# A gated recurrence feeding an ELU layer: ELU and denominators moved into PSUM, and a new order of all operations

## The chip, the cores and the metric

The kernel runs on one core of a Trainium2 chip. The time is device microseconds of one execution. Engines are named as the profile names them: PE is TensorE's matmuls (PEld its weight loads), DVE is VectorE, ACT is ScalarE, POOL is GpSimd, SP issues the DMAs. PSUM is the memory that PE writes; DVE and ACT read and write it, POOL never appears with a PSUM operand in this kernel.

## The reference

Two parts follow each other. First a recurrence over 768 steps for 4 batches and 8 heads of width 40, then a feed-forward layer with ELU on the result (3072 rows of 320).

```
for t in range(S):
    m_new = max(f[t] + m, i[t])
    C = exp(f[t] + m - m_new) * C + exp(i[t] - m_new) * outer(v[t], k[t])
    n = exp(f[t] + m - m_new) * n + exp(i[t] - m_new) * k[t]
    m = m_new
    y[t] = sigmoid(o[t]) * (C @ q[t]) / max(abs(n @ q[t]), 1)
h = x @ w_in                                  # x is y, [3072, 320]; w_in [320, 2048]
g = where(h > 0, h, exp(min(h, 0)) - 1)       # ELU
out = g @ w_out                               # [2048, 320]
```

## The kernel before, in words

The recurrence is computed in chunks. A tile is one batch and 128 steps, so there are 24 tiles, numbered n. For a tile, DVE scans the gates into decay weights (`ws`, line 509), PE multiplies keys and queries into the PSUM tile `pa` (`kq`, line 527) and forms the new state there (`us`, line 538), the weights and the product are multiplied (`wp`, 553), the state C is shrunk and added to (`shrink` 565, `gather` 571), and PE sums the outputs into the PSUM tile `pb` (`y`, line 587). Four multiplications with both inputs in SBUF prepare this: `va` (477), `kw` (513), `qb` (548, 551) and `shrink` (565). Each may stand on DVE or on POOL.

Then comes the denominator chain of a tile, on 128x8 elements: `den` takes the absolute value from `pb` (616 on ACT, 618 on DVE), `recip` inverts it (622), `half` caps it (624, DVE or POOL), `oscale` multiplies the output gate by it (626, DVE), and `result` multiplies `pb` by that into `xf` (632). PE turns `xf` (`turn`, 651) and ACT and DVE split it into an upper part `xh` (654) and a rest `xl` (656). In the kernel before, the denominators lie in two SBUF tiles, `den`.

The feed-forward layer works on blocks of two tiles (256 rows). The 2048 columns are taken 256 at a time, which makes a group: h is 128x512 in one of two PSUM banks `ph`. PE forms it with 16 matmuls (line 690), ACT writes relu(-h) and exp of it into the SBUF tile `e` (698, 700), DVE makes the ELU of it (`elu`, 702), a copy rounded to the narrower type goes to `gh` (line 201 on ACT, DVE or POOL), the rest to `gl` (707, DVE or POOL), and 12 matmuls (717) sum gh and gl times the second weights into the banks `pc`. There are 97 groups, two of them half as wide. There are 2 `e`, 3 `gh` and 2 `gl` tiles.

The weights arrive as 64-bit words and are split by a chain of DVE, ACT and POOL operations (lines 294 to 339, `join` on POOL at 325), 18 conversions in all, beside the first tiles.

Every operation is recorded by name with what it reads and writes. The table `PLACES` holds one number for each operation, its place in the order, and a letter (p, v, a, g, s for PE, DVE, ACT, POOL, SP) where it does not stand on the first engine of its list. Operations are issued in that order, so that each engine runs its own in that order, and waits come from what is read and written.

Of the kernel before, what the change touches and what calls it, by code (L numbers as in the profile page):

```python
# [11 lines left out]
F32 = mybir.dt.float32  # L12
F32R = mybir.dt.float32r
AF = mybir.ActivationFunctionType
ALU = mybir.AluOpType
# [12 lines left out]
    9g 39 0 10 3 4 5 20 30 13 59 62 61 65 64 69 73 79 2 31 46 35 48 41 51 63v 75 33 28 102v 104 92 106 105 109 116  # L28
# [13 lines left out]
    162 161 152 147 142 192 188 224v 212 199 216g 222 228 246 258 242v 254 266v 297 264 279v 281 283g 288 300 302a  # L42
    305 322 333 245 240 198 205 236 203 248 276 329 294 306 309 313 321 326 314v 331 367v 375 339 351v 354 356g
    358 361 363a 369 372 381 201 269 384g 388g 360g 400 418 373 420 442 447 489 473 390 415a 392 399 408 412 421
    452 470 492 499 406 413 432 436 458 478 483g 503 513 430 435 482 487 496 501 507 519 522 469 484 495 498 502
    516g 520 545 550 571 574 568 736 251 318 253 315 239 328 320 355v 376 368 377g 383 387 411 404 380 393 405 409
    417 426 427 429g 431 434 438a 441 448 455 342 337 330 323 335 403 394 402v 480 414 422g 423 425 466 449 450
    456 530v 536 475 488v 490 491 494 500 504 510 514 518 526 529 538 541 547 553 570 578 584 535 542 546 549 552
    562v 575 593 597 554 559 583 586 596 599 606 626 630 564 572 580 589 598 617 624 635 639 661 666 652v 835 600
    609 620 634 638 640 651g 685 691 616 623 645 647 650 665 688g 698 705 656 664 675 679 692 714 727 785 789 671  # L50
    680 693 696 699 723 732 794 800 764 812 840 718 808 832 709 719 740 749 756 788g 796 821 827 738 745 751 753
    769 795 811g 833 838 763 768 801 805 810 813 848 853 869 777 782 819 822 841 844 858 872 875 859 882 884 857
    880 943 816 842 851 870 874 876v 878g 892 896 846 849 863 867 877 883g 886g 899 902 881 885 894 898 901 906v
# [771 lines left out]
```

## Time and profile before

| what | us |
|---|---|
| median of 3 runs | 483.02 |
| lowest and highest run | 481.78, 485.48 |
| the profiled execution, its own time | 480.93 |
| span of its trace | 479.1 |

The trace is of the profiled execution. Its span leaves out 1.83 us of that execution's own time, and the median of the runs is 2.09 us above it. A busy PE in the profile is not PE at its peak, because the records of matmuls that wait in its queue overlap.

### The profile page before, as it was taken

The page shows a single profiled execution, that of the slowest core. Times are in us where ns is not written, and L with a number is a line of the kernel's source. Part 1 is how long each engine was busy: PE and PEld are TensorE (multiplying, and loading weights), DVE is VectorE, ACT ScalarE, POOL GpSimd, SP SyncE. Part 2 cuts the span into 40 slices and gives each one's busy share as a digit, 9 for nine tenths or more (in the row PEclk, how much of TensorE's full clock was granted, in tenths as well). Part 3 has the DMA queues.
Part 4 walks back from the last instruction along what each step waited for, and adds up shares of the span by engine and source line. Part 5 has one row for each costly group of instructions (what it writes and reads, how often), then busy time and mean ns, then how long its engine had stood idle before and what let it go on. Part 6 is the DMA issues. An engine that isn't in the chain of part 4 may idle for free.

```text
span 479.1 us, 14899 instructions
## 1 busy us (share of the span) xinstructions
PE 451.7 (94%) x6414; PEld 430.6 (90%) x6414; DVE 304.9 (64%) x570; ACT 224.5 (47%) x431; POOL 149.7 (31%) x167
## 2 busy tenths in 40 slices
PE   5888999998797899999999999999999999999996
PEld 2557989897797899999999999999999999999996
DVE  6868998998999665555744574464554663533342
ACT  4356896686755323434544244244342524234342
POOL 3334333453334314023132420402431424232121
PEclk9999999999997999999999999999999999999999
DMA  8963867494756250423433322016025100000000
GB/s 238 297 167 113 228 176 207 140 263 143 218 145 175 57 161 29 102 70 79 119 101 81 97 80 72 30 33 171 1 71 152 63 30 1 30 1 1 29 1 27
DMA packets 23139, 50.34 MB, mean 105 GB/s; under 512 B 4490, under 2 KB 10826, under 8 KB 23074
## 3 DMA queue, kind: packets, MB, share of 16 engines
q1 hardware_dynamic: 23074, 49.40, 36.7%
q8 instruction: 50, 0.82, 0.7%
q14 instruction: 15, 0.12, 0.1%
HBM read 43.32 MB, written 6.06 MB: 103 GB/s over the span
## 4 chain that ended last, share of the span: by engine, by line
PE 69%; DVE 4%; issue 3%; ACT 1%; POOL 0%; DVEq 0%; POOLq 0%; ACTq 0%
PE ph L690 32%; PE pc L717 29%; PE pb L587 4%; PE pa L527 2%; PE pa L538 2%; PE pb L651 1%; DVE e L702 1%; DVE gl L707 1%; DVE w L509 0%; DVE vko L513 0%; DVE vko L626 0%; DVE w L339 0%; ACT e L700 0%; POOL C L565 0%; DVE va L477 0%
## 5 line engine op out<-in xcount | busy, mean ns | idle before, releaser
L690 PE MATMUL ph<-xh,w 128*128 128x256 f32 x960 | 187.7, 288 | 1.3 <-DVE e L702 1.3
L717 PE MATMUL pc<-w,gh 128*128 128x320 f32 x768 | 172.1, 311 | 0.0
L690 PEld LDWEIGHTS ph<-xh,w 128*128 128x128 f32 x960 | 150.0, 194 | 2.7 <-DVE e L702 1.6
L717 PEld LDWEIGHTS pc<-w,gh 128*128 128x128 f32 x768 | 126.5, 188 | 0.5
L690 PE MATMUL ph<-xl,w 128*128 128x256 f32 x576 | 124.8, 285 | 0.0
L702 DVE SCALAR_TENSOR_TENSOR e<-e,ph 128x512 f32<-128x512 f32 (+1 forms) x97 | 65.5, 678 | 90.9 <-ACT e L700 90.7
L717 PE MATMUL pc<-w,gl 128*128 128x320 f32 x384 | 118.7, 309 | 0.4 <-DVE gl L707 0.4
L698 ACT ACTIVATE e<-ph 128x512 f32<-128x512 f32 (+1 forms) x97 | 57.1, 591 | 128.0 <-PE ph L690 110.8
L690 PEld LDWEIGHTS ph<-xl,w 128*128 128x128 f32 x576 | 97.8, 194 | 0.0
L717 PEld LDWEIGHTS pc<-w,gl 128*128 128x128 f32 x384 | 72.1, 188 | 0.7 <-DVE gl L707 0.7
L707 POOL TENSOR_TENSOR gl<-e,gh 128x512 fp32r<-128x512 f32 (+1 forms) x36 | 47.9, 1332 | 65.1 <-PE pc L717 29.4
L700 ACT ACTIVATE e<-e 128x512 f32<-128x512 f32 (+1 forms) x97 | 60.3, 627 | 2.4
L707 DVE TENSOR_TENSOR gl<-e,gh 128x512 fp32r<-128x512 f32 (+1 forms) x61 | 45.0, 739 | 12.2 <-POOL gh L201 3.8
L325 POOL TENSOR_TENSOR narrow<-narrow,wide 128x512 int32<-128x512 int32 (+1 forms) x18 | 27.4, 1522 | 49.7 <-ACT wide L313 18.6
L201 ACT CAST gh<-e 128x512 fp32r<-128x512 f32 (+1 forms) x48 | 29.3, 611 | 27.4 <-DVE e L702 23.8
L201 POOL CAST gh<-e 128x512 fp32r<-128x512 f32 (+1 forms) x27 | 19.3, 714 | 64.6 <-DVE e L702 62.2
L587 PE MATMUL pb<-va,w 64*32 64x41 f32 (+1 forms) x1440 | 25.3, 205 | 2.2 <-issue 2.2
L509 DVE TENSOR_TENSOR_SCAN w<-w,ones 128x512 f32<-128x512 f32 x20 | 24.5, 1228 | 2.7 <-DMA w<-f_d 2.7
L656 DVE TENSOR_TENSOR xl<-pb,xh 128x384 fp32r<-128x384 f32 x24 | 13.3, 554 | 19.0 <-ACT xh L654 19.0
L587 PEld LDWEIGHTS pb<-va,w 64*32 64x32 f32 (+1 forms) x1440 | 21.6, 112 | 3.7 <-issue 2.5
L654 ACT CAST xh<-pb 128x384 fp32r<-128x384 f32 x24 | 11.4, 474 | 27.1 <-PE pb L651 14.8
L527 PEld LDWEIGHTS pa<-qk 40*64 40x64 f32 x768 | 15.4, 145 | 8.4 <-issue 5.1
(92 smaller groups left out, 444.7 us busy)
## 6 DMA issues: line engine op xcount, KB each, us to landing
vko<-in_vko SPq DMA_DIRECT2D x24, 480.0 KB, 5.4
qk<-in_qk SPq DMA_DIRECT2D x44, 192.0 KB, 5.4
wide<-in_w_out SPq DMA_DIRECT2D x8, 640.0 KB, 5.9
w<-f_d SPq DMA_DIRECT2D x40, 128.0 KB, 3.5
wide<-in_w_in SPq DMA_DIRECT2D x8, 512.0 KB, 4.1
out<-os SPq DMA_DIRECT2D x24, 160.0 KB, 3.3
bb<-b_d SPq DMA_DIRECT2D x37, 96.0 KB, 3.4
sum<-os SPq DMA_DIRECT2D x12, 160.0 KB, 4.6
```

Of the source, the lines that this page charges most:

```text
L201: nc.scalar.copy(o, i) if e == "ACT" else eng[e].tensor_copy(o, i)
L325: lambda e: nc.gpsimd.tensor_add(word, word, high if by_act else low),
L509: lambda e: nc.vector.tensor_tensor_scan(flat, src, ones.rearrange("p h t -> p (h t)"), 0.0, op0=ALU.mult, op1=ALU.add),
L527: nc.tensor.matmul(pp()[HALF[s], two, j, :], kt[rows, j, HALF[s]], qt[rows, j, HALF[s]], start=True, stop=True, skip_group_check=True)
L587: nc.tensor.matmul(y[at, two, j, :], a, m, start=(at.start, two) not in begun, stop=False, skip_group_check=True)
L656: lambda e: nc.vector.tensor_sub(xl[j][:, :, ts], tp, xh[j][:, :, ts].bitcast(F32)),
L690: nc.tensor.matmul(h, a[g][:, cols], m, start=(i == 0), stop=(i == len(prods) - 1), skip_group_check=True)
L698: lambda e, h=h, ev=ev: nc.scalar.activation(ev, h, AF.Relu, scale=-1.0), KHP, (KE,))
L700: lambda e, ev=ev: nc.scalar.activation(ev, ev, AF.Exp, scale=-1.0), (), (KE,))
L702: lambda e, h=h, ev=ev: nc.vector.scalar_tensor_tensor(out=ev, in0=ev, scalar=-1.0, in1=h, op0=ALU.add, op1=ALU.max),
L707: lambda e, gh=gh, gl=gl, ev=ev: eng[e].tensor_sub(gl, ev, gh.bitcast(F32)),
L717: nc.tensor.matmul(pc[a][:, 0:DM], x[:, sl], bw[g][:, j, :], start=(f == f0 and part == 0), stop=(f == f1 - 1 and part == 2))
```

## The change

Three things are changed. The ELU is written over h in PSUM instead of into `e`, and `gh` and `gl` are made from there, so that neither can stand on POOL. The denominators lie in eight columns of `pb` instead of SBUF, so that `half` can't stand on POOL either; `pb` is declared as one row of 1024 columns for that, with the same addresses for all that was in it. [...]

```diff
 PLACES = """
-    9g 39 0 10 3 4 5 20 30 13 59 62 61 65 64 69 73 79 2 31 46 35 48 41 51 63v 75 33 28 102v 104 92 106 105 109 116
+    3g 6 0 4 9v 25 17 7 5 29 48 67 59 73 70 75 80 89 36 92v 94 84 96 95 100 108 117 43 38 113 120 115 122 118 124
...
-    pb = psum.tile([P, 2, 512], F32, name="pb")
+    pb = psum.tile([P, 1024], F32, name="pb")
...
-        den, xf = dens[n % room["den"]], xfs[n % room["xf"]]
-        KDN, KXF = ("den", n % room["den"]), ("xf", n % room["xf"])
+        den, xf = pb[:, 896 : 896 + H].rearrange("p (a j) -> p a j", a=2), xfs[n % room["xf"]]
+        KDN, KXF = ("den", 0), ("xf", n % room["xf"])
...
-        op(f"half {n}", "DVE POOL",
-           lambda e: eng[e].tensor_scalar(den, den, 1.0, 0.5, op0=ALU.min, op1=ALU.mult), (), (KDN,))
+        op(f"half {n}", "DVE",
+           lambda e: nc.vector.tensor_scalar(den, den, 1.0, 0.5, op0=ALU.min, op1=ALU.mult), (), (KDN,))
...
             op(f"elu {label}", "DVE",
                lambda e, h=h, ev=ev: nc.vector.scalar_tensor_tensor(
-                   out=ev, in0=ev, scalar=-1.0, in1=h, op0=ALU.add, op1=ALU.max),
-               KHP, (KE,))
-            op(f"gh {label}", "ACT DVE POOL", lambda e, gh=gh, ev=ev: copy(e, gh, ev), (KE,), (KG,))
-            op(f"gl {label}", "DVE POOL",
-               lambda e, gh=gh, gl=gl, ev=ev: eng[e].tensor_sub(gl, ev, gh.bitcast(F32)),
-               (KE, KG), (KL,))
+                   out=h, in0=ev, scalar=-1.0, in1=h, op0=ALU.add, op1=ALU.max),
+               (KE,), KHP)
+            op(f"gh {label}", "ACT DVE", lambda e, gh=gh, h=h: copy(e, gh, h), KHP, (KG,))
+            op(f"gl {label}", "DVE",
+               lambda e, gh=gh, gl=gl, h=h: nc.vector.tensor_sub(gl, h, gh.bitcast(F32)),
+               KHP + [KG], (KL,))
```

With the new letters, of the 97 groups DVE makes gl for all (61 before, POOL 36) and gh for 37 (22 before), ACT gh for 60 (48 before) and POOL none (27 before). POOL's list falls from 171 rows to 91, DVE's grows from 572 to 636.

The first place is DVE at the denominators of tile 8. `den_112` is an SBUF tile, `pb` and `ph` are PSUM, `e`, `gh`, `gl` and `vko` are SBUF. Before:

```order
L618 TENSOR_SCALAR den_112<-pb 128x8
L622 RECIPROCAL den_112<-den_112 128x8
L624 TENSOR_SCALAR den_112<-den_112 128x8
L626 SCALAR_TENSOR_TENSOR vko_106<-vko_106,den_112 128x320
L702 SCALAR_TENSOR_TENSOR e_123<-e_123,ph_147 128x512
L632 TENSOR_TENSOR xf_114<-pb,vko_106 128x320
L702 SCALAR_TENSOR_TENSOR e_124<-e_124,ph_148 128x512
L707 TENSOR_TENSOR gl_128<-e_123,gh_126 128x512
```

And in the changed kernel, at the same rows of the list:

```order
L618 TENSOR_SCALAR pb<-pb 128x8
L622 RECIPROCAL pb<-pb 128x8
L624 TENSOR_SCALAR pb<-pb 128x8
L299 TENSOR_SCALAR narrow_98<-narrow_98 128x512
L626 SCALAR_TENSOR_TENSOR vko_106<-vko_106,pb 128x320
L632 TENSOR_TENSOR xf_112<-pb,vko_106 128x320
L571 TENSOR_TENSOR C_85<-C_85,pa 104x164
L707 TENSOR_TENSOR gl_126<-ph_145,gh_124 128x512
```

The scaling of the gate and the rest of a group each had two SBUF inputs and now have one; the rest follows the denominators with other work between.

The second place is POOL in the stage of the first tiles. `vko_...<-vko,w` is kw, `C<-C,bb` is shrink, `qk<-bb,qk` is qb, `narrow` is join. Before:

```order
L513 TENSOR_TENSOR vko_106<-vko_106,w_109 128x320
L624 TENSOR_SCALAR den_111<-den_111 128x8
L325 TENSOR_TENSOR narrow_98<-narrow_98,wide_94 128x512
L565 TENSOR_TENSOR C_85<-C_85,bb_92 104x164
L325 TENSOR_TENSOR narrow_97<-narrow_97,wide_95 128x512
L707 TENSOR_TENSOR gl_129<-e_124,gh_125 128x512
L325 TENSOR_TENSOR narrow_98<-narrow_98,wide_96 128x512
L201 COPY xf_114<-xf_114 128x64
L201 CAST gh_127<-e_124 128x512
```

And in the changed kernel, as far into the conversions:

```order
L512 TENSOR_TENSOR vko_106<-vko_106,w_109 128x320
L382 TENSOR_TENSOR fi_100<-fi_100,mx 32x128
L324 TENSOR_TENSOR narrow_98<-narrow_98,wide_94 128x512
L201 COPY xf_111<-xf_111 128x64
L565 TENSOR_TENSOR C_85<-C_85,bb_92 104x164 x2
L324 TENSOR_TENSOR narrow_97<-narrow_97,wide_95 128x512
L551 TENSOR_TENSOR qk_89<-bb_92,qk_89 104x512
L512 TENSOR_TENSOR vko_107<-vko_107,w_110 128x320
L476 TENSOR_TENSOR va_86<-vko_107,va_86 128x8x40
```

Denominators, rests and copies of groups have left POOL, and the multiplications of the recurrence (kw, shrink, qb, va) stand there in their stead.

The third place is PE at the tenth turn (line 651, tile 9). Lines 690 and 717 are the first and the second layer. Before:

```order
L690 MATMUL ph_147<-xh_116,w_67 128x256
L690 MATMUL ph_147<-xl_120,w_67 128x256 x2
L690 MATMUL ph_147<-xh_116,w_67 128x256 x3
L651 MATMUL pb<-ident,xf_114 128x128 x3
L527 MATMUL pa<-qk_89 64x64 x16
L538 MATMUL pa<-va_86,vko_106 64x41 x16
L690 MATMUL ph_148<-xh_116,w_67 128x256
```

And in the changed kernel:

```order
L717 MATMUL pc_147<-w_71,gh_125 128x320 x2
L717 MATMUL pc_147<-w_71,gl_127 128x320
L717 MATMUL pc_148<-w_71,gh_125 128x320 x2
L717 MATMUL pc_148<-w_71,gl_127 128x320
L538 MATMUL pa<-va_86,vko_106 64x41 x16
L651 MATMUL pb<-ident,xf_112 128x128 x3
L690 MATMUL ph_145<-xh_114,w_67 128x256
L690 MATMUL ph_145<-xl_118,w_67 128x256
```

A group of the first layer that stood ahead of the turn now stands behind it, and the state products of tile 10 (538), which stood behind it, stand ahead; their `kq` (527) stands a few rows further ahead.

## Rows read from the trace of the kernel before

**Rows 1.** The page: busy us, share and instructions; granted clock in 40 slices.

```profile
PE 451.7 (94%) x6414; PEld 430.6 (90%) x6414; DVE 304.9 (64%) x570; ACT 224.5 (47%) x431; POOL 149.7 (31%) x167
...
PEclk9999999999997999999999999999999999999999
```

**Rows 2.** Windows: length, busy us (and instructions) of PE, PEld, DVE, ACT, POOL; clock, DMA.

```profile
0.00:55.00 55.00, 43.52 (x665) 32.33 (x666) 42.79 (x89) 29.54 (x62) 19.93 (x27) 1.00 0.72 207
55.00:146.00 91.00, 84.50 (x1469) 80.07 (x1467) 86.51 (x155) 68.55 (x131) 35.78 (x35) 1.00 0.68 190
146.00:476.00 330.00, 323.69 (x4285) 318.18 (x4284) 175.61 (x328) 126.42 (x239) 93.97 (x106) 0.99 0.23 65
```

**Rows 3.** Timeline of DVE, the tenth xl (start, us, line, operation).

```profile
144.91 0.54 DVE L656 TENSOR_TENSOR xl<-pb,xh 128x384 fp32r<-128x384 f32 x1
```

**Rows 4.** Groups of DVE by form, 0 to 146 us: busy us, mean ns, idle before.

```profile
L702 DVE SCALAR_TENSOR_TENSOR e<-e,ph 128x512 f32<-128x512 f32 x20 | 13.4, 678 | 0.3 <-ACT e L700 0.2
L707 DVE TENSOR_TENSOR gl<-e,gh 128x512 fp32r<-128x512 f32 x17 | 12.7, 758 | 0.0
...
L626 DVE SCALAR_TENSOR_TENSOR vko<-vko,den 128x320 f32<-128x320 f32 x10 | 9.3, 933 | 0.8
L553 DVE TENSOR_TENSOR w<-pa,w 128x512 f32<-128x512 f32 x11 | 7.5, 685 | 1.3 <-PE pa L538 1.3
...
L339 DVE SCALAR_TENSOR_TENSOR w<-narrow,w 128x512 fp32r<-128x512 f32 x8 | 5.9, 737 | 0.0
...
L571 DVE TENSOR_TENSOR C<-C,pa 104x164 f32<-104x164 f32 x17 | 5.3, 313 | 0.7 <-PE pa L538 0.7
...
L477 DVE TENSOR_TENSOR va<-vko,va 128x320 f32<-128x320 f32 x10 | 4.8, 476 | 0.0
L300 DVE TENSOR_SCALAR narrow<-narrow 128x512 f32<-128x512 f32 x10 | 4.7, 468 | 0.0
L513 DVE TENSOR_TENSOR vko<-vko,w 128x320 f32<-128x320 f32 x7 | 4.3, 621 | 0.1
L551 DVE TENSOR_TENSOR qk<-bb,qk 104x512 f32<-104x512 f32 x5 | 3.4, 683 | 0.0
...
L565 DVE TENSOR_TENSOR C<-C,bb 104x164 f32<-104x164 f32 x8 | 3.1, 387 | 0.0
...
L624 DVE TENSOR_SCALAR den<-den 128x8 f32<-128x8 f32 x4 | 1.8, 458 | 0.1
...
L618 DVE TENSOR_SCALAR den<-pb 128x8 int32<-128x8 int32 x4 | 0.6, 160 | 2.4 <-PE pb L587 2.4
```

**Rows 5.** Tile den over the whole span: min/median/max ns, first and last start.

```profile
L626 DVE SCALAR_TENSOR_TENSOR vko<-vko,den x24: 484/493/2824, 18.8 to 433.8; 128x320 f32<-128x320 f32 x24
...
L624 DVE TENSOR_SCALAR den<-den x15: 161/172/1308, 18.5 to 433.3; 128x8 f32<-128x8 f32 x15
```

**Rows 6.** Groups of POOL, 0 to 146 us: busy us, mean ns, idle before.

```profile
L513 POOL TENSOR_TENSOR vko<-vko,w 128x320 f32<-128x320 f32 x5 | 5.9, 1183 | 6.9 <-DVE w L509 3.5 <-PE pb L651 3.3
```

**Rows 7.** Groups of ACT by form, whole span: busy us, mean ns, idle before.

```profile
L700 ACT ACTIVATE e<-e 128x512 f32<-128x512 f32 x95 | 59.4, 631 | 2.3
L698 ACT ACTIVATE e<-ph 128x512 f32<-128x512 f32 x95 | 56.3, 595 | 124.6 <-PE ph L690 107.7 <-DVE gl L707 7.4 <-issue 5.2
L201 ACT CAST gh<-e 128x512 fp32r<-128x512 f32 x47 | 28.9, 615 | 26.9 <-DVE e L702 23.3 <-PE pc L717 1.9 <-PE pb L587 1.5
```

**Rows 8.** The chain that ended last, in order of time: start, us, what.

```profile
177.07 0.62 PE pa L527 x32
177.70 0.45 PE pa L538 x32
...
188.67 3.84 PE ph L690 x32
192.51 3.52 PE pc L717 x24
```

**Rows 9.** Timeline of PE: the longest stop in its own issuing.

```profile
151.90 0.59 PE L527 MATMUL pa<-qk 40*64 40x64 f32 x11 [2.87 <-issue]
```

More of the change, by code (lines that the diff above doesn't have):

```diff
@@ new lines @@
+    1036 1038 1040 1044a 1046 1050 1055 690 772 775g 786g 782g 828 833 1052 839 840 844 841 911 1062 1088 1226
+    1230 1233 1234 1236 1238v 1241 1270 1273 1232 1242 1250 1252 1266 1268v 1272 1275 1283 1260 1263 1269 1271
+    1274 1276 1277 1288 1304 1278 1281 1284 1289 1291 1297 1302 1310 1320 1293 1300 1306 1308 1312 1316 1318 1324
+    1336 1314 1317 1321 1323 1325 1328 1330 1340 1343 1326 1329 1332 1333 1335 1338v 1341 1359 1364 1331 1334 1337
+    1339 1342 1344 1346 1370 1376 1382 1394 1384 1388 866 905 903 909 963 838 984 923v 1032 1009 1020 935 1025
@@ new lines @@
+    1494 1527 1569 1593 1607 1609 1610 1612 1615v 1618 1629 1635 1608 1611 1614 1616 1619 1623 1627 1659 1662 1620
+    1624 1631 1634 1636 1640v 1643 1664 1668 1644 1648 1652 1656 1661 1663v 1665 1671 1686 1651 1667 1669 1670
+    1672 1675 1681 1689 1701 1673 1676 1680 1684 1694 1697 1700 1704 1710 1693 1698 1702 1703 1705 1707 1709 1713
+    1723 1706 1708 1711 1712 1714 1716 1719 1725 1727 1731v 1734 1730 1732 1360 1389 1372 1377 1375 1292 1307
+    1449v 1547 1433 1460 1469 1471 1559 1557 1522v 1526 1575 1579 1580 1590 1591 1592 1595v 1598 1600 1638 1519
@@ new lines @@
+    1516 1431 1418 1485 1403 1401 1461v 1467 1501 1561 1573 1574 1603 1630 1429v 1576 1641 1645 1646 1647 1649
+    1650 1653v 1658 1660 1666 1715 1718 1721 1722 1724 1726v 1728 1739 1743 1720 1729 1735 1736 1738 1741v 1744
+    1746 1751 1733 1737 1740 1742 1747 1750v 1753 1756 1763 1748 1754 1757 1758 1760 1762 1764 1767 1775 1759 1761
+    1765 1766 1768 1771v 1773 1779 1784 1769 1772 1777 1782 1785 1788v 1791 1794 1801 1789 1792 1795 1796 1798
+    1800 1802 1805 1807 1797 1799 1803 1804 1806 1808v 1810 1812 1819 1824 1826 1823v 1828 1476 1528 1531 1483
@@ new lines @@
+    1480 1628 1525 1633v 1683 1554 1566 1637 1639 1642 1657 1654v 1655 1685 1687v 1688 1690 1691 1692 1695a 1696
+    1699 1745 1578 1586 1596 1582 1584 1632 1562 1677v 1717 1674 1678 1679 1682 1749 1755 1752v 1770 1774 1776
+    1778 1780 1781 1783 1786 1787 1790 1793 1809 1811 1813 1814 1816 1818 1820 1831 1835 1815 1817 1821 1825 1829
+    1830v 1833 1837 1839 1822 1827 1832 1834 1836 1838v 1840 1848 1851 1841 1842 1844 1845 1847 1849 1852 1854
+    1865 1843 1846 1850 1853 1855 1857v 1858 1869 1872 1856 1859 1861 1862 1864 1867v 1870 1874 1877 1860 1863
@@ L107 @@
+    1866 1868 1871 1873 1875 1883 1887 1876 1878 1879 1881 1882v 1884 1890 1880 1885 1886 1888 1889v 1891 1892
+    1894 1896 1893 1895
 """
@@ L193, in tile_mlstm_then_elu_ffn @@
     room = dict(
-        wide=3, narrow=2, gates=2, qk=3, bb=3, vko=3, w=3, den=2, xf=2, x=4, e=2, gh=3, gl=2, os=3,
+        wide=3, narrow=2, gates=2, qk=3, bb=3, vko=3, w=3, xf=2, x=4, e=2, gh=3, gl=2, os=3,
     )
@@ L234, in tile_mlstm_then_elu_ffn @@
     ws = tiles("w", P, H, Q)
-    dens = tiles("den", P, 2, HH)
     xfs = tiles("xf", P, 3 * P if XDUP else H * D)
@@ L519, in us @@
             return pa[:, s, HH * Q : HH * (Q + E)].rearrange("p (j e) -> p j e", e=E)
-        y = pb[:, :, 0 : HH * E].rearrange("p a (j e) -> p a j e", e=E)
+        part = pb[:, 0:1]
+        y = bass.AP(tensor=part.tensor, offset=part.offset, ap=[list(part.ap[0]), [512, 2], [E, HH], [1, E]])
         def products(e):
```

129 lines of the change are left out of this document (56 added, 73 removed), and 11 rows, old and new, of the table PLACES.

## The prediction, made before the changed kernel was run

> **What bounds the kernel now.** I read the page first, then windows by stage, then DVE's groups in the stage where DVE is full. The page has PE at 94% and DVE at 64% of the span [rows 1], which alone says that nothing on DVE matters. The windows say otherwise [rows 2]. Up to 55 us the first four tiles pass through a chain of all engines. From 55 to 146 us DVE is busy 86.51 of 91.00 us, so it idles 4.5 us in all: it is the engine that sets when this stage ends. From 146 to 476 us PE is busy 323.69 of 330.00 us and DVE only 175.61: PE sets the pace there. So time can be won in two places only: by DVE's queue up to some 146 us, and by PE's few stops behind. As the mark at which the first stage ends I take the tenth xl (tile 9): it starts at 144.91 us and lasts 0.54 [rows 3], so it ends at 145.5; the span ends 333.6 us later.
>
> What fills DVE ahead of the mark is in rows 4. The oscale instruction (line 626) stands out: 933 ns in the mean of ten, where the median over the whole trace is 493 and the longest 2824 [rows 4, 5]. Its inputs are both in SBUF, and so are those of gl (line 707), 758 ns, while wp (line 553), of the same size with one input in PSUM, takes 685 and elu (line 702) 678. I read the long ones as DVE waiting for POOL, which works beside it on SBUF.
>
> **The change, part by part, up to the mark.** The sum is made against the profiled execution.
>
> 1. Long instructions that become short. With the denominators in PSUM, oscale has one SBUF input left, gl has one, and half (line 624) none. I price each at its undisturbed time: oscale 10 x (933 - 493) = 4.4 us; gl 17 x (758 - 685) = 1.2; half 4 x (458 - 172) = 1.1 [rows 4, 5]. Together 6.8 us to rounding. Below, the gain is 0, if the same waiting moves to DVE's other instructions; above, it is what else waits besides, some 0.5 us for line 339 (8 x (737 - 678) by elu's time of the same width) [rows 4]. I take 6.8, since the forms with a PSUM input are even: 678 and 685 are within 1% of each other.
>
> 2. Work moved from DVE to POOL ahead of the mark, counted in the two orders: va 10 to 4, kw 7 to 2, qb 7 to 4, shrink 10 to 4. At the rows' means that is 6 x 0.476 + 5 x 0.621 + 3 x 0.683 + 6 x 0.387 = 10.3 us less [rows 4].
>
> 3. Work moved to DVE or drawn ahead of the mark: half 4 to 10 (6 x 0.172 = 1.0), den 4 to 7 (0.5), gl 17 to 19 (1.4), two instructions of the setup that POOL did (1.4, at line 553's 685 each), hi 1 to 3 and clip 17 to 18 (3 x 0.468 = 1.4), lo 18 to 19 (0.7), wp 10 to 11 (0.7), gather 16 to 18 (0.6), one gh that reads PSUM (0.3 more); elu goes 20 to 19 (0.7 less) [rows 4, 5]. That is 7.3 us more. A few gate operations also leave DVE; they would only add to the gain, and I leave them out. With step 2: 3.0 us less.
>
> 4. Writing to PSUM with DVE occurs nowhere in the trace: elu, recip, half and den now do it. Reading PSUM costs nothing that the rows show (553 against 551, 685 to 683 [rows 4]). Below I put no cost. Above, each of the 46 instructions ahead of the mark that now write there (19 elu, 7 den, 10 recip, 10 half) is longer by a whole small instruction, 160 ns (line 618) [rows 4]: 7.4 us. I take 0, the row nearest by form being the reading one. [...] A dear PSUM is a rival below.
>
> 5. PE. Ahead of the tenth turn stand 336 matmuls of line 690 and 216 of 717 before, and 320 and 216 now; one tile's kq and us have come ahead instead. At 3.84 us for 32 of line 690, and 0.62 + 0.45 for kq and us [rows 8], PE has 1.92 - 1.07 = 0.85 us more left behind the mark.
>
> 6. What is late next. When DVE runs faster it meets waits that its own queue hid. In the order now, kw, qb, shrink and va stand on POOL, where kw took 1183 ns in this stage against DVE's 621 [rows 4, 6], and gather, us and y wait for them. I let DVE idle two thirds as much again as the 4.5 us of rows 2, 3 us. The bounds are 0 and the whole gain.
>
> 7. Behind the mark. DVE gets all of gl and 37 gh: 36 gl from POOL at 685, and gh at 685 where it reads PSUM, some 35 us over the run. With 175.61 of 330 us busy [rows 2] there is room, DVE would reach about 64%. I put it at nothing; the cover is PE's own work between one group and the next, and the rival on the banks says what it costs where that is gone.
>
> The sum: 145.5 - 6.8 - 3.0 + 3.0 = 138.7 for the mark; 333.6 + 0.85 behind it: 473.2 of span. The profiled execution is 1.83 us above its span, and the median of the runs 2.09 above that: 477.1. So 477 us, 6 less than 483.02. A measurement of this kernel tells about 1% from no change, which is 4.8 us: 478.2 and 487.8 are the borders.
>
> **The rivals.**
>
> The gain is whole, and PE's stops go too. [...] 477.1 - 3.0 - 2.9 - 3.6 = 467.6. For it: these stops wait for nothing that the profile shows, so a new order may miss them. Against: as many small matmuls of the recurrence are issued in a row as before.
>
> The contention stays. POOL has 70 operations ahead of the mark where it had 56, and more of them with two SBUF inputs (kw 9, qb 6, shrink 13, va 7, against 5, 3, 7, 2), and DVE still has the joins' neighbours (line 339 and its like) and the scans with two. If what oscale lost is lost there, 477.1 + 6.8 = 483.9: no change. Against: fewer such instructions stand on DVE.
>
> PSUM operands are dear. With the upper bound of step 4, 46 x 160 ns in DVE's full stage, 477.1 + 7.4 = 484.5: no change. For it: no row shows DVE writing PSUM. Against: the rows that read it are even. [...]
>
> Slower: PE waits for its two banks. A bank ph was free once elu had read it; now gh and gl read it too, so the first layer of the group after next waits for relu, exp, elu, gh and gl: 0.595 + 0.631 + 0.678 + 0.615 + 0.685 = 3.2 us [rows 4, 7], some 3.5 with the way between the engines. In the order now, PE has at least 16 matmuls of line 690 and 12 of 717 between, 1.92 + 1.76 = 3.68 us [rows 8]; ten of the 95 pairs have under 4.0 us and 24 under 4.7. One instruction of 0.685 us in DVE's queue ahead of gl makes such a pair late. If all 24 lose that, it is 16.4 us and 493.5; it decides from 0.45 us in each of the 24 (10.8 us) on. For it: all of gl and 37 gh now stand on the engine that also does the recurrence. Against: ACT and DVE idle for long in this stage before relu, 124.6 us over the run [rows 7], and PE idles 6.3 of 330 us [rows 2], so the queues are short.
>
> **How the numbers follow.** The forecast has 0.48, with its own range of 472 to 482; the whole gain 0.13; contention stays 0.17; dear PSUM 0.07; banks 0.15. Of the forecast's share I put two thirds under 478.2, with the whole gain 0.13 and a little of the others: faster 0.48. Slower takes most of the banks' share and a little of dear PSUM: 0.15. The rest, 0.37, is within 1%. The range: the whole gain's 467 below, and 488 above, which takes in contention and PSUM and leaves out most of the banks.
>
> **What would show it.** Right: oscale at about 490 ns in every tile and gl at about 685 with no long one; the tenth xl ending at 138 to 140 us; DVE idle from 55 us to it about 7 us. PE's waits for DVE or ACT behind 146 us stay under 2 us in all. Wrong: lines 308, 338 and 508 of the changed kernel grown by what 626 lost (contention); elu, recip and half longer than 0.69, 0.2 and 0.17 us (PSUM); line 690 waiting for gl (line 707) behind 146 us (banks); DVE idle behind POOL's kw or qb by more than 5 us (step 6). If the tenth xl comes early and the end does not, the loss lies in PE's stage, and steps 5 and 7 are wrong.

## The result, and the profile after

The changed kernel takes 461.53 us in the median of 4 runs (459.75 to 465.34), the kernel before 483.86 beside it: a ratio of 0.9551, 95% interval 0.9479 to 0.9623. The forecast was 477.0 us with a range of 467 to 488: 22 us are gone where 6 were forecast, and the range missed. The profiled execution took 459.75 us, the fastest of the four, 458.0 of it span. One run of e6 below, 473.82 us at a mean granted clock of 0.981, belongs to a slower state than all others and is left out.

The page first (busy time of each engine, and the granted clock in 40 slices), which answers to [rows 1]:

```profile
PE 443.9 (97%) x6414; PEld 423.7 (93%) x6414; DVE 328.4 (72%) x634; ACT 233.7 (51%) x444; POOL 66.3 (14%) x90
...
PEclk9999999999999999999999999999999999999999
```

PE is busy for 7.8 us less with the same 6414 matmuls. The slice at the lower clock is gone in this execution. POOL has less than half its work. The windows (length; busy us and instructions of PE, PEld, DVE, ACT, POOL; clock, DMA share, GB/s), which answer to [rows 2]:

```profile
0.00:55.00 55.00, 49.06 (x812) 37.47 (x813) 47.19 (x102) 32.95 (x70) 19.93 (x34) 1.00 0.84 225
55.00:146.00 91.00, 88.90 (x1563) 85.63 (x1565) 82.86 (x159) 67.94 (x124) 44.37 (x53) 1.00 0.69 197
146.00:455.00 309.00, 305.93 (x4055) 300.58 (x4045) 198.34 (x375) 132.77 (x251) 1.95 (x3) 1.00 0.23 64
```

In the middle stretch PE is now busy 88.90 of 91.00 us where it was 84.50, and DVE 82.86 where it was 86.51: PE is now the fuller of the two. (The tenth xl now ends at 132.7 us, so the stretch holds some of the next stage.) In the first 55 us, which the prediction left alone, PE does 5.5 us more than before.

The mark, the tenth xl, in DVE's timeline (start, length), which answers to [rows 3]:

```profile
132.15 0.56 DVE L656 TENSOR_TENSOR xl<-pb,xh 128x384 fp32r<-128x384 f32 x1
```

It ends at 132.7 instead of 145.5 us; forecast were 138.7. Windows up to the mark, of the kernel before:

```profile
0.00:145.45 145.45, 127.47 (x2127) 112.03 (x2128) 128.76 (x242) 97.54 (x192) 55.16 (x62) 1.00 0.69 195
55.00:145.45 90.45, 83.95 (x1465) 79.70 (x1464) 85.96 (x154) 68.00 (x130) 35.23 (x35) 1.00 0.68 189
```

and of the changed kernel:

```profile
0.00:132.70 132.70, 124.67 (x2116) 110.40 (x2117) 117.79 (x236) 94.41 (x182) 55.55 (x77) 1.00 0.78 218
55.00:132.70 77.70, 75.60 (x1306) 72.93 (x1305) 70.60 (x135) 61.46 (x112) 35.62 (x43) 1.00 0.74 213
```

DVE's work to the mark falls from 128.76 to 117.79 us, 11.0 less. Its idle time is the rest of each window: 12.2 us in the first 55 before [rows 2] and 7.8 now, 4.5 behind them before and 7.1 now. What DVE waits for from 55 us to the mark in the changed kernel (us in total, times, longest):

```profile
DVE ph L702 <- ACT e L700: 1.8, 3, 0.8
DVE w L553 <- PE pa L538: 1.7, 1, 1.7
DVE gl L707 <- ACT gh L201: 1.0, 2, 0.7
DVE narrow L299 <- ACT narrow L293: 0.6, 2, 0.4
DVE C L571 <- POOL C L565: 0.2, 1, 0.2
```

DVE's groups by form up to 133 us (busy us, mean ns, idle before), which answer to [rows 4, 5]:

```profile
L702 DVE SCALAR_TENSOR_TENSOR ph<-e,ph 128x512 f32<-128x512 f32 x19 | 13.1, 690 | 2.4 <-ACT e L700 2.2
L707 DVE TENSOR_TENSOR gl<-ph,gh 128x512 fp32r<-128x512 f32 x19 | 13.0, 685 | 1.5 <-ACT gh L201 1.2
...
L338 DVE SCALAR_TENSOR_TENSOR w<-narrow,w 128x512 fp32r<-128x512 f32 x8 | 5.6, 697 | 0.0
...
L626 DVE SCALAR_TENSOR_TENSOR vko<-vko,pb 128x320 f32<-128x320 f32 x10 | 4.9, 487 | 0.5
...
L624 DVE TENSOR_SCALAR pb<-pb 128x8 f32<-128x8 f32 x10 | 1.7, 173 | 0.3
```

oscale takes 487 ns in the mean where it took 933, gl 685, half 173, and elu, which now writes to PSUM, 690 where it took 678. POOL's kw (line 512) answers to [rows 6]:

```profile
L512 POOL TENSOR_TENSOR vko<-vko,w 128x320 f32<-128x320 f32 x9 | 6.9, 765 | 9.2 <-DVE w L508 4.4 <-DVE pb L624 3.6 <-DVE pb L618 1.2
```

Its mean fell from 1183 to 765 ns. Last, the chain of the changed kernel, which answers to [rows 8] (start, us, what), and all waits of PE behind 146 us, which answer to [rows 9] (us in total, times, longest):

```profile
179.33 3.77 PE ph L690 x32
...
204.58 3.64 PE ph L690 x32
...
316.57 3.63 PE ph L690 x32
```

```profile
PE pa L538 <- issue: 1.2, 2, 1.0
PE ph L690 <- DVE gl L707: 1.1, 1, 1.1
```

The stop of 2.87 us is gone. And something that was not meant to change is faster: 32 matmuls of the first layer took 3.83 or 3.84 us in the chain before, everywhere, and take 3.63 to 3.9 now. The time from the start of one matmul to the start of the next is called its step here. Over all pairs of neighbours in the trace that are under 200 ns apart, the step of line 690 fell from 119.8 to 115.6 ns, that of line 717 stayed (146.8 and 146.7).

Behind the mark, all steps add up as follows (us; from the trace's start times; a stop is a step over 0.45 us in the two layers, over 0.3 us elsewhere):

```
                         before   changed
from L690 to L690         138.6     133.9
from L717 to L717         129.5     130.0
stops                       6.9       3.0
all other steps            54.6      54.4
last start to the end       4.0       4.1
mark to the end           333.6     325.3
```

So the stretch behind the mark is 8.3 us shorter, where 0.85 longer was forecast: 4.7 us come off line 690 and 3.9 off the stops. A part of line 690's row is the clock. From within its stop of 2.87 us on, the kernel before ran 6.8 us at the lower of the clock's two levels in its trace, 1.00 and 0.50 (window as above):

```profile
150.40:157.20 6.80, 5.30 (x63) 5.23 (x64) 5.18 (x9) 1.51 (x3) 2.96 (x3) 0.50 0.35 101
```

The 14 steps of the group of line 690 in it took 213 or 214 ns each, 1.3 us more than at 120.

### The profile page after: what moved, and what is told of

The parts are those of the page before. It is cut to its first block, busy times and chain, and to the rows that moved or that the text cites. A ratio compares the mean times of both kernels' runs of the same rounds, so it can differ in the third digit from the quotient of the medians.

```text
span 458.0 us, 14815 instructions
## 1 busy us (share of the span) xinstructions
PE 443.9 (97%) x6414; PEld 423.7 (93%) x6414; DVE 328.4 (72%) x634; ACT 233.7 (51%) x444; POOL 66.3 (14%) x90
## 4 chain that ended last, share of the span: by engine, by line
PE 91%; DVE 3%; issue 2%; ACT 2%; DMA 2%; POOL 1%; SPq 0%; ACTq 0%; DVEq 0%; POOLq 0%
PE ph L690 38%; PE pc L717 35%; PE pb L587 7%; PE pa L527 3%; PE pa L538 3%; PE pb L651 2%; DMA vko<-in_vko 1%; PE ph L485 1%; PE pc L485 1%; POOL narrow L324 1%; DVE xl L656 0%; PE pc L491 0%; DMA fi<-in_gates 0%; ACT e L698 0%; ACT xh L654 0%
## 5 line engine op out<-in xcount | busy, mean ns | idle before, releaser
L690 PE MATMUL ph<-xh,w 128*128 128x256 f32 x960 | 182.4, 283 | 1.1 <-DVE gl L707 1.1
L690 PEld LDWEIGHTS ph<-xh,w 128*128 128x128 f32 x960 | 146.3, 190 | 2.6 <-DVE gl L707 1.6
L690 PE MATMUL ph<-xl,w 128*128 128x256 f32 x576 | 121.3, 281 | 0.2 <-DVE xl L656 0.2
L702 DVE SCALAR_TENSOR_TENSOR ph<-e,ph 128x512 f32<-128x512 f32 (+1 forms) x97 | 66.5, 686 | 60.4 <-ACT e L700 60.0
L690 PEld LDWEIGHTS ph<-xl,w 128*128 128x128 f32 x576 | 95.3, 190 | 0.4 <-DVE xl L656 0.4
L707 DVE TENSOR_TENSOR gl<-ph,gh 128x512 fp32r<-128x512 f32 (+1 forms) x97 | 66.3, 683 | 28.2 <-ACT gh L201 20.1
L201 ACT CAST gh<-ph 128x512 fp32r<-128x512 f32 x60 | 35.2, 586 | 32.2 <-DVE ph L702 31.0
L201 DVE CAST gh<-ph 128x512 fp32r<-128x512 f32 (+1 forms) x37 | 25.0, 676 | 1.1
L527 PE MATMUL pa<-qk 40*64 40x64 f32 x768 | 18.6, 236 | 2.1 <-DVE xl L656 1.5
```

What stands on the lines that cost most here:

```text
L201: nc.scalar.copy(o, i) if e == "ACT" else eng[e].tensor_copy(o, i)
L527: nc.tensor.matmul(pp()[HALF[s], two, j, :], kt[rows, j, HALF[s]], qt[rows, j, HALF[s]], start=True, stop=True, skip_group_check=True)
L690: nc.tensor.matmul(h, a[g][:, cols], m, start=(i == 0), stop=(i == len(prods) - 1), skip_group_check=True)
L702: lambda e, h=h, ev=ev: nc.vector.scalar_tensor_tensor(out=h, in0=ev, scalar=-1.0, in1=h, op0=ALU.add, op1=ALU.max),
L707: lambda e, gh=gh, gl=gl, h=h: nc.vector.tensor_sub(gl, h, gh.bitcast(F32)),
```

## The experiments

All ratios are to the kernel before, run beside each kernel on the same chip; the chips differ from group to group, so ratios and not times are compared. The table has the measured times, the mean step of the first layer's matmuls, and the starts of the fourth and the tenth xl (xl 3 and xl 9) in one profiled execution; "x - w1" is the distance of the two operands of that layer in SBUF, modulo 256 bytes.

```
kernel                      us     ratio [95%]              step ns  x-w1  xl 3  xl 9
before                    483.86   1                         119.8     0   50.6  144.9
changed                   461.53   0.9551 [0.9479, 0.9623]   115.6   192   45.7  132.2
e1_before_shifted         479.08   0.9906 [0.9880, 0.9933]   117.2    64   50.6  146.6
e8_before_shifted_192     477.40   0.9879 [0.9841, 0.9917]   115.2   192   50.9  147.6
e2_after_unshifted        466.31   0.9646 [0.9608, 0.9684]   119.8     0   46.5  133.0
e5_address_table          462.41   0.9559 [0.9520, 0.9599]   117.7   all   46.0  132.0
e9_fine_table             461.0    (one run)                 118.2   all   45.8  131.2
e12_all_shifted_128       461.07   0.9559 [0.9506, 0.9613]   115.6   192   45.6  131.1
e4_den_alone              477.46   0.9865 [0.9818, 0.9912]   119.8     0   50.9  142.1
e10_before_den_shifted    472.22   0.9779 [0.9729, 0.9830]   115.1   192   50.2  143.1
e3_order_alone            474.06   0.9784 [0.9726, 0.9842]   117.2    64   47.3  138.6
e11_order_and_address     467.80   0.9689 [0.9634, 0.9745]   115.4   192   46.6  137.5
e6_elu_in_psum_only       464.59   0.9627 [0.9572, 0.9681]   115.5   192   46.7  134.9
e7_den_in_psum_only       460.85   0.9527 [0.9483, 0.9570]   115.4   192   48.9  135.8
e13_moves_to_pool_undone  467.97   0.9655 [0.9581, 0.9730]   115.5   192   48.1  137.2
e14_setup_on_pool         460.99   0.9555 [0.9489, 0.9621]   115.9   192   49.1  134.5
e15_changed_again         458.69   0.9508 [0.9467, 0.9549]   115.4   192   44.9  129.7
e16_den_only_again        460.28   0.9534 [0.9497, 0.9570]   115.5   192   49.3  136.8
```

### Why the first layer's step fell

The two den tiles held 64 bytes per partition together. Without them every later tile in SBUF moved by 64 bytes: x, which line 690's matmuls of 256 columns read, but not w1, of which its weight loads (PEld, 128x128 each) read. Theory A blames that, theory B the order or the quieter SBUF. The first two runs shift the tiles alone, in either kernel:

```
+    pad = const.tile([P, 16], F32, name="pad")
     xfs = tiles("xf", P, 3 * P if XDUP else H * D)
```

> The kernel before, its order and its code untouched, with an unused tile of 64 bytes per partition put ahead of the xf tiles, so that xf, xh, xl, e, gh, gl and os lie 64 bytes further on, at the addresses (taken modulo 128) that they have in the changed kernel, where the two den tiles of 64 bytes together are gone. Theory A (the address of the first layer's moving operand sets its step): the mean step from one L690 matmul to the next falls from 119.8 ns to about 115.5 ns, as in the changed kernel, and the time by up to 1536 x 4.3 ns = 6.6 us, to 477 to 479 us. Theory B (the step fell because the new order or the PSUM writes leave SBUF quieter): the step stays at 120 ns and the time at 483.9 us, within 1%.

> The changed kernel with the same unused 64 bytes ahead of xf, which puts the later tiles back at the addresses modulo 128 that they have before. Theory A: the step of L690 goes from 115.5 back to 120 ns, and the time from 461.5 to 466.5 to 468 us (1216 to 1536 steps of 4.3 ns). Theory B: the step stays at 115.5 ns and the time at 461.5 us.

With 64 unused bytes and nothing else, the kernel before is 0.94% faster, and the changed kernel loses 0.95% of the time before (the intervals of these two, up to 0.9623 and from 0.9608, just meet; the step is the clearer sign). The chain of e1_before_shifted:

```profile
181.07 3.77 PE ph L691 x32
188.37 3.63 PE ph L691 x32
```

and of e2_after_unshifted, back at what was before:

```profile
183.02 3.83 PE ph L691 x32
...
208.63 3.83 PE ph L691 x32
```

Theory B falls. But e1 shows 117.2 ns, not 115.5. Its x tiles are at 192 modulo 256, those of the changed kernel at 64; so place or distance had to be told apart by more addresses. e8 puts 192 bytes ahead of xf in the kernel before; e5 has a 64-byte tile ahead of every w1, w2, xh and xl but the first of each:

```
+    def apart(name, *shape, n):
...
+            if j:
+                const.tile([P, 16], F32, name=f"pad{name}{j}")
+            made.append(const.tile(list(shape), F32R, name=f"{name}{j}"))
...
-    xh = tiles("xh", P, 3, TMAX * L, dt=F32R, n=room["x"])
+    xh = apart("xh", P, 3, TMAX * L, n=room["x"])
+    const.tile([P, 16], F32, name="padx")
```

> The kernel before with 192 unused bytes ahead of xf, so that its x tiles lie at 64 modulo 256, as in the changed kernel (with 64 bytes they lay at 192). Address modulo 256: step 115.7 ns, 1.5 ns less than with 64 bytes, and 476.5 us. If the changed kernel's lower step needs its order or its PSUM writes too: 117.2 ns and 479 us.

> The changed kernel with unused 64-byte tiles between the four w1 tiles, the four w2 tiles, the four xh and the four xl, so that the addresses modulo 256 of w1 0 to 3 are 128, 192, 0, 64, of w2 0 to 3 are 64, 128, 192, 0 and of xh and xl 0 to 3 are 192, 0, 64, 128 (in the changed kernel: 128 for all of w1 and w2, 64 for all x). One run so gives the step of both layers at each address. If the address of the moving operand modulo 256 sets the step, L690 shows 119.8 ns for x at 128, 117.2 at 192, 115.7 at 64, whatever w1 is, and something unknown, 113 to 120, at 0; and L717, whose moving operand is w2 and which takes 146.7 ns with w2 at 128, falls by 2.5 to 4 ns for the w2 tiles at 192 and 64. If it is the distance between the two tiles that are read together, the table of L690 changes with x minus w1. If it is another thing that the shift moved, the table is flat. Time: the mean over the addresses, 461 to 465 us.

e8 shows 115.2 ns and 477.40 us, as theory A had it, with the order and all writes of before:

```profile
184.05 3.64 PE ph L691 x32
191.20 3.65 PE ph L691 x32
```

The table of e5 (mean step of line 690's matmuls, ns; rows: address of x, columns: address of w1, both modulo 256):

```
          w1 at 128   192     0     64
x at 192     117.8  119.5  114.4  118.6
x at   0     118.3  116.3  119.2  114.8
x at  64     117.9  119.1  116.3  119.5
x at 128     119.6  115.4  118.5  117.7
```

Read along the diagonals, it is a table of the distance: x - w1 of 0 gives 119.5, 64 gives 117.0, 128 gives 118.6, 192 gives 115.6 (each the mean over its four cells, 315 to 331 steps). One cell does not fit: x at 64 with w1 at 128 shows 117.9, and the same pair 115.6 in the changed kernel, where all w1 lie alike. Single cells scatter: the changed kernel has one distance throughout, and its 16 pairs of tiles give 114.1 to 116.4 ns. Line 717 took 146.1 to 146.9 ns in all its 16 cells, so the second layer doesn't care, for which I have no reason. The last two runs look for a better place: e12 moves all large tiles by 128 bytes together (a 128-byte tile ahead of w1), e9 goes in steps of 32:

```
+    pad = const.tile([P, 32], F32, name="pad")
     w1 = [const.tile([P, 5, G * P], F32R, name=f"w1{g}") for g in range(NF // G)]
```

```
+    xh = apart("xh", P, 3, TMAX * L, gaps=(0, 32, 128, 64))
+    xl = apart("xl", P, 3, TMAX * L, gaps=(32, 32, 128, 64))
...
+    ghs = apart("gh", P, 512, gaps=(0, 32, 32))
```

> The changed kernel with 128 unused bytes ahead of w1, so that all large tiles move together: w1 at 0 and x at 192 modulo 256, their distance still 192. If the distance alone counts: L690 at 115.7 ns and 461.5 us. If the place itself counts too, as the one cell of the address table with w1 at 0 and x at 192 hints (114.4 ns): 1.3 x 1536 = 2 us less, 459.5 us.

> The changed kernel with unused tiles of 32, 128 and 64 bytes between the four xh and the four xl and of 32 bytes between the three gh, so that x minus w1, modulo 256, is 192, 224, 96 and 160 for the four x buffers and w2 minus gh is 96, 64 and 32 for the three gh buffers. By the table of the run before (distance 0: 119.5 ns, 64: 116.3 to 117.8, 128: 118.3 to 119.1, 192: 114.4 to 115.4), L690 shows 115 to 116 ns at 192. If the distance sets the step bit by bit, 160 and 224 lie between their neighbours, 116 to 118 ns, and 96 about 118; if only multiples of 64 decide, 224 is like 192 (115) and 96 like 64 (117). L717 stays at 146.7 ns at every distance if only the first layer is sensitive.

e12 gives 115.6 ns and the time of the changed kernel, so at this second place too the distance counts. In e9 the distances 160, 192, 224 and 96 gave 118.4, 116.3, 118.4 and 120.0 ns: odd multiples of 32 are no better than bad ones of 64. The changed kernel has the best distance that was tried; nothing in its diff aims at that.

### Denominators, ELU and order

e4 is the kernel before with the denominators in PSUM (so half stands on DVE for all 24 tiles) and the den tiles replaced by unused bytes, so that PE's operands stay where they were:

```
-    dens = tiles("den", P, 2, HH)
+    pad = const.tile([P, 16], F32, name="pad")
...
-        den, xf = dens[n % room["den"]], xfs[n % room["xf"]]
+        den, xf = pb[:, 1, 384 : 384 + H].rearrange("p (a j) -> p a j", a=2), xfs[n % room["xf"]]
```

> The kernel before with the denominators kept in PSUM and nothing else of the change: half on VectorE all 24 times, an unused 64 bytes in the place of the den tiles, so that no other tile moves. By the prediction's step 1, oscale falls from 933 to 493 ns in 10 of its cases and half no longer waits for POOL: up to 4.4 us less on VectorE ahead of the tenth xl, which ends 3 to 4 us earlier, and 480 us. If what oscale loses is taken back by POOL or by waits: 483.9 us. Both theories of the step want 120 ns here, since no address that PE reads moves and the order is that of before.

477.46 us, 1.35% less, and 2.5 us under the better of the two times expected: step 1 of the prediction without its gl, in the order of before. In the profile DVE's work ahead of the tenth xl is 3.8 us less, where oscale and half were priced at 5.5, and the xl comes 2.8 us earlier. The mean granted clock of e4's runs was 0.992 to 0.996, against 0.986 to 0.989 in the kernel before beside it, so what of the 6.2 us is step 1 alone is not shown. oscale in that run (min/median/max ns):

```profile
L626 DVE SCALAR_TENSOR_TENSOR vko<-vko,pb x24: 478/486/489, 18.8 to 431.2; 128x320 f32<-128x320 f32 x24
```

The longest is 489 ns where it was 2824 [rows 5]. What made it long can be read from the trace of before: each of the eight oscale over 550 ns starts while POOL is inside an instruction with SBUF operands and ends 347 to 356 ns after one of POOL's ends; the other sixteen take 484 to 495 ns and overlap none. The other half of the pair is the new order without any edit of the code, e3 with the distance of e1 and e11 with that of the changed kernel (`PLACES` of the changed kernel in the kernel before, and 64 or 192 unused bytes ahead of xf):

> The kernel before with the order of the changed kernel and nothing else of the change (ELU written to SBUF, denominators in SBUF), and with the 64 bytes, so that its x tiles lie where they lie in the changed kernel. If the order carries the gain: 461 to 465 us, the tenth xl at 132 to 135 us, in spite of oscale that takes 900 ns beside POOL. If the PSUM edits carry it (step 1 of the prediction, 6.8 us of VectorE time ahead of the tenth xl): the tenth xl at 137 to 140 us and 467 to 470 us. Theory A wants an L690 step of 115.5 ns here too, theory B (in its form that the PSUM writes do it) 120 ns.

> The order of the changed kernel and its addresses (x minus w1 192 modulo 256), but ELU in SBUF and denominators in SBUF as before. With the run where the x tiles lay 64 bytes off it (474.1 us, step 117.2 ns), the address alone is worth 1.9 x 1536 = 2.9 us: 471 us. [...]

Against the kernel before at the same distance the order alone is worth 0.9906 - 0.9784 = 1.2% (e1, e3) and 0.9879 - 0.9689 = 1.9% (e8, e11), 6 to 9 us. The fourth xl starts 3.3 to 4.3 us earlier with it, and DVE is idle 7.9 us (e3) and 7.3 us (e11) in the first 55 us, where it was 12.2 in the kernel before. The window of e11:

```profile
0.00:55.00 55.00, 48.02 (x805) 36.22 (x806) 47.75 (x98) 32.46 (x69) 23.03 (x34) 1.00 0.86 223
```

e3 was slower than either of its two expectations. Its longest oscale is still 2694 ns, and e11's 2684, so the order alone does not take POOL's hold away. Now one edit at a time in the changed kernel, e6 with den back in two SBUF tiles (and 192 unused bytes, which keep the distance), e7 with the ELU lines of before:

```
+    dens = tiles("den", P, 2, HH, n=2)
+    pad = const.tile([P, 48], F32, name="pad")
...
+        den, xf = dens[n % 2], xfs[n % room["xf"]]
```

```
-                   out=h, in0=ev, scalar=-1.0, in1=h, op0=ALU.add, op1=ALU.max),
-               (KE,), KHP)
+                   out=ev, in0=ev, scalar=-1.0, in1=h, op0=ALU.add, op1=ALU.max),
+               KHP, (KE,))
...
+               lambda e, gh=gh, gl=gl, ev=ev: eng[e].tensor_sub(gl, ev, gh.bitcast(F32)),
```

> The changed kernel with the denominators back in two SBUF tiles and unused bytes behind them, so that the x tiles are at the same address modulo 256 as in the changed kernel; ELU stays in PSUM, the order stays. Step 1 of the prediction: the lines on the denominator lengthen again where POOL works beside them, oscale from 490 to up to 933 ns in 6 to 10 cases, so the tenth xl comes 3 to 4 us later (132.2 to 136) and the time is 465 us. If the den edit brings nothing once the order is new: 461.5 us.

> The changed kernel with ELU written to SBUF as before (gh and gl read it there), denominators still in PSUM, order and addresses of the changed kernel. If the ELU edit has no price and no gain of its own ahead of the tenth xl (step 4 of the prediction): 461 to 463 us, gl back from 683 to about 410 ns on VectorE. If the PSUM write is what shortens the step of L690 beyond the address: step 117 ns and 465 us. [...]

e6 loses 0.76% (the intervals of the two meet), and its oscale is long again:

```profile
L628 DVE SCALAR_TENSOR_TENSOR vko<-vko,den x24: 480/493/2692, 16.8 to 418.7; 128x320 f32<-128x320 f32 x24
```

e7 loses nothing: 0.9527 against 0.9551. Its gl, with both inputs in SBUF, took 693 ns in the median and up to 1909, not the 410 expected; in the kernel before its median was 685 too. ELU in PSUM has a price, though, that can be seen. In e2, e5, e6, e9, e12, e13, e14 and the changed kernel PE waits near 280 us for gl, which frees its bank, for 0.8 to 2.3 us; in e3, e7 and e11, which have ELU in SBUF, it does not wait there. In e12's timeline of PE:

```profile
284.72 0.39 PE L691 MATMUL ph<-xh,w 128*128 128x256 f32 x1 [2.25 <-DVE gl L708]
```

Right behind it the granted clock is at the lower of its levels, 0.50, and PE starts 15 matmuls in 3 us, then 23 (windows of e12):

```profile
286.00:289.00 3.00, 3.00 (x15) 3.00 (x14) 0.56 (x1) 1.23 (x2) 0.00 (x0) 0.50 0.00 0
289.00:292.00 3.00, 3.00 (x23) 3.00 (x22) 2.13 (x4) 0.59 (x1) 0.00 (x0) 0.94 0.00 0
```

In the changed kernel's profile the wait was 1.1 us, and the clock stayed at 1.00. DVE's own copies gh (one input) are longer too, 690 ns from PSUM in the changed kernel and 483 from SBUF in e7, in a stage where DVE has room.

As e7 showed none of it, I ran it once more beside the changed kernel itself, five rounds each:

> The changed kernel itself, as the measure for the run that follows on the same chip: 461.5 us. In every profile with ELU in PSUM PE waits once near 280 us for gl, which frees the bank (0.8 to 2.3 us); the same is expected here.

> The kernel with ELU in SBUF, denominators in PSUM and the order and addresses of the changed kernel, against the changed kernel on the same chip. If the wait for the bank near 280 us (and the lower granted clock that follows the longer ones of these waits) is the only price of ELU in PSUM, this kernel has none of it and is 1 to 2 us faster, 459.5 to 460.5; if ELU in PSUM gives as much elsewhere, both are the same, 461.5 us.

458.69 and 460.28 us, with intervals that overlap: the same. The kernel with ELU in SBUF can wait for a bank too, as e16's profile shows near 287 us; there it is elu that frees it:

```profile
PE ph L690 <- DVE e L702: 0.8, 1, 0.8
```

In both profiles its tenth xl came later (135.8 and 136.8 against 132.2 and 129.7 us). But the profiled executions of e7 and e16 were the slowest of their runs (462.26 and 464.34 us) and those of the changed kernel the fastest of theirs (459.75 and 457.61), so these starts do not compare the two kernels. No run beat the changed kernel by more than the runs differ. Do the parts add? e10 is the kernel before with denominators and distance, its order as it was:

```
-    dens = tiles("den", P, 2, HH)
...
-        den, xf = dens[n % room["den"]], xfs[n % room["xf"]]
+        den, xf = pb[:, 1, 384 : 384 + H].rearrange("p (a j) -> p a j", a=2), xfs[n % room["xf"]]
```

> The kernel before, its order untouched, with two small parts of the change: the denominators in PSUM, and with them the x tiles 64 bytes lower (x minus w1 192 modulo 256, as in the changed kernel). If the two gains found apart (6.2 us for the denominators, 6.2 for the address) add, 471 us, and what is then missing to 461.5 us is the order's with its PE stops: the stop of 2.9 us in PE's issuing near 150 us and the half clock behind it stay, since the order is that of before. If they overlap (PE waits for VectorE anyway up to the tenth xl, so the address counts only behind it): 473 us.

472.22 us, 2.2% less, where the two apart took off 1.35 and 1.2%. The interval, 0.5% to either side, holds both the whole sum and a small overlap: they add, or nearly. The stop near 150 us stays as the order of before has it, here 2.02 us in the timeline of PE:

```profile
149.35 0.39 PE L526 MATMUL pa<-qk 40*64 40x64 f32 x11 [2.02 <-issue]
```

### What in the order brings its share

The order, the third of the things changed, is the new table `PLACES`, numbers and letters. It changes more than DVE's queue. PE's stops behind the mark, counted as above, are 5.1 to 7.1 us in the five profiles in the order of before, and 2.5 to 7.9 in the thirteen in the new order (3.0 and 3.9 in the two of the changed kernel itself). The clock differs more clearly. Each of those five profiles has 6.8 to 13.6 us at the lower level, 0.50, between 126 and 172 us; of the thirteen, eight have none (apart from the last 4 us) and five have 3.4 to 6.8. Over whole runs the mean granted clock was 0.982 to 0.993 in 39 runs of the kernel before and 0.992 to 1.00 in ten of the changed kernel. Within one kernel the clock goes with several us: e3 took 468.87 us at 1.00 and 473.21 to 475.15 at 0.986 to 0.991, e15 457.61 to 458.76 at 0.996 to 1.00 and 462.99 at 0.992. So a part of the order's share comes with the clock; what in the order does it, and how much of it follows from PE's stops, is not shown.

The next two runs undo single parts of the new letters.

```
+            o.engine = "DVE" if o.name in ON_DVE else o.engine
```

This line, in Plan.run, makes e13, with 23 names (6 va, 5 kw, 4 qb, 8 shrink). e14 has the same line with "POOL" for zones and blockf 0.

> The changed kernel with the 23 operations that the new order moved from VectorE to POOL in the first twelve tiles (va 6, kw 5, qb 4, shrink 8) put back on VectorE at the same places of the order. Step 2 of the prediction prices those ahead of the tenth xl at 10.3 us of VectorE: the tenth xl would end up to 10 us later, near 142 us, and the time would be 465 to 471 us. If the new order hides them in VectorE's waits, the loss is under 3 us and the order's gain lies in the sequence and not in the engines.

> The changed kernel with the two setup operations that it moved from POOL to VectorE (the table of ones and the first block of gates) back on POOL, at the same places. If they carry the early start (first xl 21.4 us instead of 24.1, fourth 45.7 instead of 50.6), xl 0 and xl 3 return by 1 us or more and the time goes to 463 us or above; if the early start comes from the order of the conversions among the first tiles, everything stays within 0.5 us.

e13 ends 1.0% later (the intervals meet, 0.9581 against 0.9623), and its tenth xl starts 5.0 us later in the profile:

```profile
137.16 0.55 DVE L661 TENSOR_TENSOR xl<-pb,xh 128x384 fp32r<-128x384 f32 x1
```

```profile
55.00:137.70 82.70, 79.75 (x1359) 76.09 (x1355) 78.86 (x155) 65.79 (x121) 26.67 (x29) 1.00 0.74 207
```

From 55 us to its mark DVE has 78.86 us of work instead of 70.60, POOL 26.67 instead of 35.62. But the profiled run was the slowest of e13's four, and the time goes with the clock here: at 1.00 a run took 462.79 us, and at 0.985 to 0.992 the other three took 467.55 to 469.21. At 1.00, e13 is thus 2 to 4 us behind the runs of e12 and e14 at 1.00 beside it (458.51 to 460.64), and that is a single run. So the move of step 2 may bring a few us by itself; the rest of e13's loss comes with the lower clock, and why that was lower in three of its four runs is open.

e14 changes nothing in the time, and its first xl starts at 21.7 us, so the two setup operations do not carry the early first xl. Its fourth xl is late, at 49.1 us, as in e7 and e16, where those two stand as in the changed kernel; so something else varies there, and none of the three is slower for it.

## Why the prediction was wrong, point by point

- **Step 1** (long instructions become short, 6.8 us): right. Each form went to the price given for it, 487, 685 and 173 ns. The reading was also right: oscale was long because POOL held it up, as the ends of the long ones show. What the step is worth in time is less sure: 6.2 us in e4, with its higher clock. The maxima agree, 489 ns with one SBUF input (e4) and 2692 with two (e6).
- **Steps 2 and 3** (work moved, 3.0 us net): right for DVE's work. With step 1, it was to fall by 9.8 us up to the mark and fell by 11.0; with the moves undone, e13 has 8.3 us more of it from 55 us to its mark. That this work sets the time of the whole kernel is not shown by e13.
- **Step 4** (writing PSUM costs nothing): right, 690 against 678 ns for elu, and e7, e15 and e16 find no difference. The rival of dear PSUM falls.
- **Step 6** (DVE idles 3 us more from 55 us to the mark): the size came out, 4.5 to 7.1 us, "about 7" as the text had it, but by luck. The reason given was waiting for POOL's kw, qb, shrink and va; the waits above are for ACT (3.4 us) and PE (1.7), and 0.2 for POOL.
- **What was missing ahead of the mark:** a term for the first 55 us. The prediction called them a chain through all engines and then took DVE's idle time there as fixed. The new order took 4.4 us out of it, 12.2 to 7.8. With 1.2 us more of work saved and 0.4 less given back, that is the whole difference at the mark, 138.7 against 132.7. e3 and e11 show that it comes with the order alone. How much time it is worth at the end is not shown: e14 and e16, in the new order, idle 13.0 and 10.9 us there and take as long as the changed kernel.
- **Step 7** (behind the mark nothing) failed, and it is the largest miss, 9.1 us with step 5's 0.85. PE set the pace there, as it said; but "PE-bound" was taken for "fixed". Of the 8.3 us, 4.7 are the first layer's steps (the shorter step, and 1.3 us of it the group at the lower clock) and 3.9 PE's stops. The step is the den tiles' doing, in a way that had no line in the sum: 64 bytes of SBUF fewer put x at another distance from w1. e1, e2 and e8 show it. The stops are the rival that had 0.13 ("PE's stops go too"): every profile in the order of before has a stop of 2.0 to 3.6 us near 150 us in line 527 or the line that answers to it (e1, e4, e8, e10), and none in the new order has it. Stops of other lines take its place in some (1.6 us for DVE's xf in e3 and e11), so the 3.9 us hold for this pair of profiles. The 3.6 us in the sum of that rival, 467.6, from which the range has its lower end, are shown by no run: the kernel before was at 0.50 for 6.8 us there, with 1.3 us more in its 14 steps of line 690, and the changed kernel at 1.00 from 146 to 455 us.
- **The rivals.** "The contention stays" fell: line 338 (339 before) went from 737 to 697 ns, and no line grew by what 626 lost. "PE waits for its two banks" named the right wait and the wrong number: one place of 24, at 1.1 us in the profile of the changed kernel.

By parts, in medians or differences of ratios: the distance 4 to 6 us, the denominators 4 to 8, the order 6 to 12 with the higher clock that goes with it, ELU in PSUM nothing that can be told from zero. The prediction had the second, of the third the moved work alone, and not the first. The failed step is step 7, which put the stretch behind the mark at nothing beside step 5's 0.85 us; the first 55 us, held fixed, come second.

## What to carry to other kernels

When an edit adds or removes a tile, list which tiles behind it change their address, and compare the step of PE's matmuls, start to start, at both: here 64 unused bytes were worth 1% without a change to any instruction. A stage "bound by PE" is not fixed in length: add up its steps and its stops by line. And where DVE and POOL share a stage, look for instructions whose mean lies far above their median; here an operand moved to PSUM took the waiting away (489 ns at most in e4, from 2824), and a new order alone did not (2684 in e11). And before a gain is put down to an edit, compare the granted clock of the runs on both sides.

## What the runs showed of the hardware that I had not expected

- The step of line 690's matmuls, with 256 columns, went in e5 with how far their moving operand lies from the weights in SBUF, modulo 256 bytes: 119.5, 117.0, 118.6 and 115.6 ns at 0, 64, 128 and 192. That of line 717's, with 320 columns, w2 moving and gh or gl as weights, was 146 to 147 ns there at the four multiples of 64. Pairs of tiles at one distance still differ by up to 2.3 ns (114.1 to 116.4 in the changed kernel).
- At the good distance the step is not one number: in the changed kernel behind 60 us the commonest steps are 113 and 114 ns (696 of 1340) and 117 and 118 (463), and a run of 8 matmuls mostly stays with one of them. The two rows of 3.63 and 3.77 us for 32 come from that mixture. What chooses between them is open.
